# Attention and the first expert job on one core: transposes into two PSUM banks, other engines for some small steps, plain float32 in the first second layer

## The chip, the cores and the metric

The program runs on one core of one Trainium2 chip. Its time is the device time of one execution in microseconds (us), the median of several runs. Five engines work beside each other and wait for one another on semaphores: TensorE (PE in the rows; PEld is its weight load), VectorE (DVE), ScalarE (ACT), GpSimd (POOL) and SyncE (SP), which here only issues transfers.

## The reference

Three layers follow one another. Only the first, and the first job of the second, are touched by the change.

```
q, k, v: (4, 12, 448, 64) float32
q_n, k_n = rmsnorm(q, g_q), rmsnorm(k, g_k)
scores   = q_n @ k_n.T / 8;  attn = softmax(scores);  x = attn @ v     # -> (1792, 768)
expert   = argmax of x_n @ emb_n.T / tau, gate = its softmax weight    # 8 experts, top 1
x        = gate * relu(x @ w1[expert]) @ w2[expert]                    # w1: 768x1024, w2: 1024x768
out      = leaky_relu(x @ w_in) @ w_out                                # 768x2048, 2048x768, float64 weights
```

## The kernel before

All products are made to nearly float32 precision from a rounded part ("hi", type fp32r, one pass of TensorE) and a remainder ("lo"): hi*hi + hi*lo + lo*hi. Each value that enters a product is therefore copied once by ACT (hi = rounded copy) and subtracted once by DVE or POOL (lo = value - hi).

**Attention** runs over 12 pairs n (two heads, two batches) and 24 units u (one head of a pair, two batches side by side, so 896 rows of queries in seven tiles t of 128; tile 3 has 64 rows of either batch). For a pair: `load` brings q and k; `square`, `meansq`, `root` and `normalise` make the root mean square norm, mostly on POOL (the root itself is one `pow` on POOL, L280); `turn` (L322) transposes 16 tiles of 128x128 in four groups g (k and q of either batch) into PSUM tiles of one bank; `stack` makes hi (L335, L337) and lo (L339, L341) of each group; `swap` and `twice` (L352, L360) copy them by DMA so that hi and lo of a head lie above each other on 128 partitions. For the first pair the copies of the first head are made by ACT and DVE (`first_swap`, L381, L383), and unit 0 takes its third product from 64 partitions of `KL` alone (L413).

For a unit: `score` (L415) makes each tile with two products of 448 columns (four for tile 3), `rowmax` (L419, DVE) and `expo` (L425, ACT) follow; `ptrans` (L439) transposes the 28 blocks of the probabilities in eight groups g of four or three into one bank each, `psplit` makes hi (L450, ACT) and lo (L453, DVE) of each group; `pv` (L469) multiplies by v in 14 products; `evac` (L473, ACT) brings the two results to SBUF; `out_mm` (L489) turns them back and adds the expert logits, and `out_done` (L508, DVE) divides. PSUM has eight banks: two for scores, three for transposes (ring T), three for results (ring V).

**The order** of all this is written by a planner, `Order.run`: each operation has an engine, a price in ns, operations that it needs, rings of buffers that it takes and frees, and a due time (`TICKS`). The planner goes through a model of the five queues and writes the program in the order in which it would start the operations. An engine executes its instructions in that order, whatever the real times are.

**The first expert job** (`Experts.first`, also ordered by the planner) takes 128 tokens of expert 7 in four slices k of 256 hidden columns: `l1_parts` (L1204) makes x @ w1 in three parts, `relu`, a transpose (L1228), hi and lo (L1231, L1234), and `l2` (L1132, L1133) multiplies by w2 with three products per 128 hidden columns. Beside it run the routing of the second half of the tokens (L759 to L862), the gather of the rows of the next job (L1033) and their transposes (L1051). Splits of w1 and w2 run on ACT and DVE (L1015, L1017). The w1 of three slices is loaded during attention; the w2 of slices 1 to 3, and the w1 of slice 3, are loaded after attention has ended. The jobs after it (L1112 on) and the dense layer (L1626 on) have their own orders and are not touched.

Of the kernel before, what the change touches and what calls it, by code (L numbers as in the profile page):

```python
# [23 lines left out]
PS_T = 3  # L24
# [4 lines left out]
RAW = 3  # L29
TICKS = dict(start=1189.5, const=102.3, emb=15.4, max=0.4, exp=0.16, t=15.23, hi=5.93, lo=1.08, pv=30.06, ev=0.01,  # L30
             j=48.9, qk0=-40.65, qk1=-14.6, qk2=-23.81, qk3=-19.01, loadv=-29.18, v=-2.18, load=-67.34, norm=-54.47,
             root=16.77, mul=-14.43, route=2.68, droute=0.26, x0=-12.27)
# [6 lines left out]
ACTSQ = 3  # L39
WAIT = dict(PE=195, Act=140, DVE=125, Pool=70, SP=0)  # L40
# [60 lines left out]
class Attention:  # L101
    def __init__(self, tc, ctx, q, k, v, g_q, g_k, emb, tau, xtok, big, logits):
# [3 lines left out]
        self.xtok, self.big, self.logits = xtok, big, logits  # L106
# [10 lines left out]
        self.ps_v = pool("a_ps_v", 8 - PS_S - PS_T, space=PSUM)  # L117
# [4 lines left out]
    def setup(self, ident, turned):  # L122
        nc = self.nc
        self.ident, self.turned = ident, turned
# [3 lines left out]
        self.rhalf = c.tile([128, 28], F32, name="rhalf")  # L128
        nc.gpsimd.memset(self.rhalf, -0.5)
        self.KT = c.tile([128, 896], F32R, name="KT")  # L130
        self.QT = c.tile([128, 960], F32R, name="QT")
        self.QL = c.tile([128, 960], F32R, name="QL")
        for t in (self.QT, self.QL):
            nc.vector.memset(t[:, 448:512].bitcast(F32), 0.0)
        self.JE = c.tile([128, 12, 72], F32, name="JE")
        first = c.tile([128, 1], F32, name="first")
        nc.vector.memset(first, 0.0)
        nc.scalar.activation(out=first, in_=first, func=ACTF.Exp)

    def sums(self, half):  # L140

        rows = slice(half, half + 64)
        self.nc.scalar.copy(out=self.JE[rows, :, 0:64], in_=self.ident[rows, rows].unsqueeze(1).to_broadcast([64, 12, 64]))
# [13 lines left out]
    def zero_row(self):  # L157

        z = self.QT[:, 448:512].bitcast(F32)
# [3 lines left out]
    def experts(self, part):  # L163
# [20 lines left out]
        elif part == 4:  # L184
            self.emb_t = self.ps_t.tile([128, 512], F32, name="tp")
            for i in range(6):
                nc.tensor.transpose(self.emb_t[:, 8 * i:8 * i + 8], emb[:, 128 * i:128 * i + 128], self.ident[0:8, 0:8])
        else:
            je = self.JE.rearrange("p (i j) c -> p i j c", j=2)
            for a in (0, 64):  # L190
                for b in (0, 64):
                    nc.vector.tensor_copy(je[b:b + 64, :, a // 64, 64:72],
                                          self.emb_t[a:a + 64, 0:48].rearrange("p (i e) -> p i e", e=8))


    def load(self, n, i, part):
# [7 lines left out]
        if part == 1:  # L204
            for b in range(2):
                (nc.sync if n or i else nc.gpsimd).dma_start(out=qk[b * 64:b * 64 + 64, i + 6:i + 8, :],
# [6 lines left out]
    def load_v(self, n):  # L213
# [3 lines left out]
        vn = self.p1.tile([128, 16, 64], F32, name="vn")  # L217
        for b in range(2):
            nc.sync.dma_start(
                out=vn[:, b * 6:b * 6 + 6, :].rearrange("p (h r) d -> p h (r d)", r=3),  # L220
                in_=self.v[2 * bp + b, h0:h0 + 2, 0:384, :].rearrange("h (p r) d -> p h (r d)", r=3))
            for half in (0, 64):
                nc.sync.dma_start(
                    out=vn[half:half + 64, 12 + 2 * b:14 + 2 * b, :],
                    in_=self.v[2 * bp + b, h0:h0 + 2, 384:448, :].rearrange("h p d -> p h d"))
        self.pair[n]["vn"] = vn

    def split_v(self, n, part):
        nc = self.nc
        pr = self.pair[n]  # L230
        vn = pr["vn"]
        if part == 0:
            pr["vs"] = self.p2.tile([128, 16, 128], F32R, name="vs")
            nc.scalar.copy(out=pr["vs"][:, :, 0:64], in_=vn)
        else:
            s = slice(8 * part - 8, 8 * part)
            nc.gpsimd.tensor_tensor(out=pr["vs"][:, s, 64:128], in0=vn[:, s, :], in1=pr["vs"][:, s, 0:64].bitcast(F32),
# [9 lines left out]
    def square(self, n, a, b):  # L247
        nc = self.nc
        pr = self.pair[n]
        if "sq" not in pr:  # L250
            pr["sq"] = self.big("sq").rearrange("p (g d) -> p g d", d=64)
            for name in "ryzh":
                pr[name] = self.p2.tile([128, 28], F32, name="rstd" + name)
# [6 lines left out]
    def meansq(self, n, a, b):  # L260
# [4 lines left out]
        if n > 0:  # L265
# [6 lines left out]
    def root(self, n, a, b, k):  # L272
# [3 lines left out]
        if k > 11:  # L276
            if k == 12:
                self.nc.gpsimd.tensor_scalar(out=r, in0=r, scalar1=64e-6, scalar2=None, op0=ALU.add)
            else:
                self.nc.gpsimd.tensor_tensor(out=y, in0=r, in1=self.columns(self.rhalf, a, b), op=ALU.pow)  # L280
            return
# [25 lines left out]
    def turn(self, n, g):  # L307
# [4 lines left out]
        if g == 0:  # L312
            pr["KL"] = self.p2.tile([128, 896], F32R, name="KL")
        b, q = divmod(g, 2)
        base = 0 if q else 14
        ps = pr["t", g] = self.ps_t.tile([128, 512], F32, name="tp")
        o = 64 if g == 3 else 0

        last = [(base + 6, 0 if g == 3 else 384, self.turned if b else self.ident)]
        tiles = [(base + b * 8 + 2 * r, o + 128 * r, self.ident) for r in range(3)]  # L320
        for j, c, unit in last + tiles if g == 3 else tiles + last:
            nc.tensor.transpose(ps[:, c:c + 128], qk[:, j:j + 2, :].rearrange("p h d -> p (h d)"), unit)  # L322

    def stack(self, n, g, part):
        nc = self.nc
        pr = self.pair[n]
        ps = pr["t", g][:, 0:448]
        b, q = divmod(g, 2)
        if q:
            hi, lo = [t[:, 512 * b:512 * b + 448] for t in (self.QT, self.QL)]  # L330
        else:
            hi, lo = [t[:, 448 * b:448 * b + 448] for t in (self.KT, pr["KL"])]
# [1521 lines left out]
```

## Time and profile before

| | |
|---|---|
| median of 3 runs | 1159.12 us (1153.48 to 1159.16) |
| the profiled execution: its own time | 1154.31 us |
| its span, first to last instruction | 1152.4 us |
| TensorE busy | 1112.6 us, 97% |
| VectorE, ScalarE, GpSimd busy | 71%, 59%, 44% |
| attention, first score to last `out_mm` | 17.0 to 321.0 us |
| first expert job, to the first product of the next | 321.0 to 349.2 us |

How to read it: a busy PE is not PE at its peak, since the time of a product counts from its start to its modelled end, and products overlap. What a product costs in a stream is the step from one start to the next.

### The profile page before, as it was taken

The page shows a single profiled execution, that of the slowest core. Times are in us where ns is not written, and L with a number is a line of the kernel's source. Part 1 is how long each engine was busy: PE and PEld are TensorE (multiplying, and loading weights), DVE is VectorE, ACT ScalarE, POOL GpSimd, SP SyncE. Part 2 cuts the span into 40 slices and gives each one's busy share as a digit, 9 for nine tenths or more (in the row PEclk, how much of TensorE's full clock was granted, in tenths as well). Part 3 has the DMA queues.
Part 4 walks back from the last instruction along what each step waited for, and adds up shares of the span by engine and source line. Part 5 has one row for each costly group of instructions (what it writes and reads, how often), then busy time and mean ns, then how long its engine had stood idle before and what let it go on. Part 6 is the DMA issues. An engine that isn't in the chain of part 4 may idle for free. (4 is left out here: it accounts for less than half of the span.)

```text
span 1152.4 us, 19036 instructions
## 1 busy us (share of the span) xinstructions
PE 1112.6 (97%) x6863; PEld 985.0 (85%) x6863; DVE 813.1 (71%) x1354; ACT 681.3 (59%) x1346; POOL 501.4 (44%) x453
## 2 busy tenths in 40 slices
PE   5899999999989999999999999999999999999998
PEld 2789899899878999899899888888888888888997
DVE  5789898998877777877877779999933333323443
ACT  6889898799855665765856744544433332333453
POOL 6889898694211010201111156786683121221242
PEclk9999999999989999999999999999999999999999
DMA  7789988878487868977978655686543225323452
GB/s 156 168 187 216 203 204 191 182 175 213 129 278 262 302 227 285 328 249 259 359 254 282 221 193 207 204 300 241 213 165 138 97 80 180 110 83 109 166 192 83
DMA packets 155422, 233.09 MB, mean 202 GB/s; under 512 B 60286, under 2 KB 117886, under 8 KB 155326
## 3 DMA queue, kind: packets, MB, share of 16 engines
q1 hardware_dynamic: 151422, 215.75, 61.1%
q0 software_dynamic: 2784, 12.93, 3.5%
q10 hardware_dynamic: 1120, 3.16, 0.8%
q8 instruction: 56, 0.92, 0.3%
q14 instruction: 40, 0.33, 0.1%
HBM read 169.24 MB, written 30.81 MB: 174 GB/s over the span
## 5 line engine op out<-in xcount | busy, mean ns | idle before, releaser
L1604 POOL TENSOR_TENSOR w1l<-c,w1h 128x768 fp32r<-128x768 f32 x44 | 90.0, 2056 | 112.8 <-ACT w1h L1602 112.8
L1668 DVE SCALAR_TENSOR_TENSOR g<-hps,hs 128x512 f32<-128x512 f32 (+1 forms) x64 | 39.8, 621 | 134.9 <-ACT hs L1667 134.8
L1604 POOL TENSOR_TENSOR w2l<-c,w2h 128x768 fp32r<-128x768 f32 x42 | 88.6, 2119 | 91.7 <-ACT w2h L1602 87.6
L1667 ACT COPY hs<-hps 128x512 f32<-128x512 f32 (+1 forms) x64 | 34.1, 533 | 157.6 <-PE hps L1662 154.4
L419 DVE TENSOR_REDUCE negm<-S 128x1 f32<-128x448 f32 x165 | 101.5, 616 | 22.8 <-PE S L415 21.6
L1132 PE MATMUL ya<-w2h,QB 128*128 128x512 f32 x288 | 113.2, 404 | 0.5 <-ACT QB L1231 0.5
L425 ACT ACTIVATE P<-S,negm 128x448 f32<-128x448 f32 x165 | 105.4, 640 | 11.3 <-DVE negm L419 7.6
L450 ACT CAST PH<-tp 128x512 fp32r<-128x512 f32 (+1 forms) x192 | 98.2, 532 | 14.8 <-PE tp L439 13.6
L439 PE MATMUL tp<-ident,P 128*128 128x128 f32 (+1 forms) x672 | 105.3, 278 | 0.5 <-DVE PL L453 0.4
L1033 POOL DMA_INDIRECT KB<-rows,gidx x16 | 19.1, 1195 | 196.4 <-PE hps L1204 59.8
L1112 PE MATMUL hps<-xh,w1h 128*128 128x256 f32 x336 | 95.7, 285 | 1.2 <-ACT w1h L1015 1.2
L1112 PE MATMUL hps<-xh,w1l 128*128 128x256 f32 x336 | 95.1, 283 | 0.5 <-DVE w1l L1017 0.5
L1112 PE MATMUL hps<-xl,w1h 128*128 128x256 f32 x336 | 95.3, 284 | 0.3 <-DVE xl L1058 0.3
L439 PEld LDWEIGHTS tp<-ident,P 128*128 128x128 f32 (+1 forms) x672 | 81.8, 137 | 15.5 <-issue 1.3
L453 DVE TENSOR_TENSOR PL<-tp,PH 128x512 fp32r<-128x512 f32 (+1 forms) x144 | 86.8, 615 | 6.9 <-ACT PH L450 6.3
L1017 DVE TENSOR_TENSOR w1l<-qk,w1h 128x768 fp32r<-128x768 f32 x86 | 81.1, 956 | 13.9 <-ACT w1h L1015 13.5
L1669 ACT CAST gh<-g 128x512 fp32r<-128x512 f32 (+1 forms) x64 | 36.3, 568 | 81.1 <-DVE g L1668 80.2
L1133 PE MATMUL yb<-w2h,QB 128*128 128x256 f32 x288 | 81.8, 284 | 0.8 <-DVE yn L1179 0.8
L1662 PE MATMUL hps<-yh,w1h 128*128 128x512 f32 (+1 forms) x198 | 71.8, 363 | 0.1
L1662 PE MATMUL hps<-yh,w2h 128*128 128x512 f32 (+1 forms) x192 | 70.7, 368 | 1.1 <-DVE g L1668 1.1
L1662 PE MATMUL hps<-yh,w1l 128*128 128x512 f32 (+1 forms) x198 | 70.8, 358 | 0.0
L1662 PE MATMUL hps<-yl,w1h 128*128 128x512 f32 (+1 forms) x198 | 70.8, 357 | 0.0
(326 smaller groups left out, 3635.3 us busy)
## 6 DMA issues: line engine op xcount, KB each, us to landing
c<-wc SPq DMA_DIRECT2D x57, 768.0 KB, 4.6
qk<-in_moe_w SPq DMA_DIRECT2D x44, 768.0 KB, 6.8
x<-in_moe_w SPq DMA_DIRECT2D x27, 768.0 KB, 7.3
s<-in_moe_w_in SPq DMA_DIRECT2D x16, 768.0 KB, 7.7
s<-in_moe_w_out SPq DMA_DIRECT2D x16, 768.0 KB, 6.7
wc<-c SPq DMA_DIRECT2D x16, 768.0 KB, 6.1
LL<-KL SPq DMA_DIRECT2D x46, 224.0 KB, 4.5
sq<-in_moe_w SPq DMA_DIRECT2D x13, 768.0 KB, 7.4
```

Source lines behind the costliest of these rows:

```text
L419: self.nc.vector.tensor_reduce(out=un["negm"][:, t:t + 1], in_=un["S", t], op=ALU.max, axis=AXX, negate=True)
L425: self.nc.scalar.activation(out=un["P"][:, t, :], in_=un["S", t], func=ACTF.Exp, bias=un["negm"][:, t:t + 1], scale=1.0, accum_out=un["den ...
L439: nc.tensor.transpose(ps[0:m, 128 * j:128 * j + 128], P[:, t, 128 * c:128 * c + m], self.ident)
L450: nc.scalar.copy(out=hi, in_=ps)
L453: nc.vector.tensor_tensor(out=lo, in0=ps, in1=hi.bitcast(F32), op=ALU.subtract)
L1017: lo.tensor_tensor(out=t[2 * m + 1][:, s, :], in0=r, in1=hi.bitcast(F32), op=ALU.subtract)
L1112: nc.tensor.matmul(ps[:, 0:T], l, r, start=(a == 0), stop=(a == len(m) - 1))
L1132: nc.tensor.matmul(y["a"][j], l, r[:, 0:512], start=st, stop=sp)
L1133: nc.tensor.matmul(y["b"][j], l, r[:, 512:768], start=st, stop=sp)
L1604: eng.tensor_tensor(out=l, in0=c, in1=h.bitcast(F32), op=ALU.subtract)
L1662: nc.tensor.matmul(ps[:, t], l, r[:, t], start=(a == 0), stop=(a == len(m) - 1))
L1668: nc.vector.scalar_tensor_tensor(out=g, in0=ps[:, 0:T], scalar=0.01, in1=hs, op0=ALU.mult, op1=ALU.max)
```

## The change

- `turn`, `stack`, `ptrans` and `psplit` work on PSUM tiles of two banks: a pair has two groups of eight transposes instead of four of four, a unit four of seven instead of eight of four and three, and hi and lo are one instruction of up to 896 columns each. Ring T has two such tiles (four banks), ring V two banks. All transposes of a unit now need all seven tiles of its probabilities.
- The stacked q's have four fixed buffers with a zero gap; unit 0 takes its third product from a buffer `LL` of 128 partitions with zeros below, filled by two more DVE copies.
- `spin`: 23 products on zeros at the start, 3 and 1 more between the first transposes, whose result nobody reads.
- Other engines: the second evacuation of every odd unit from 5 on goes from ACT to DVE; the hi of v from ACT to POOL (not in pair 0); the mean squares and root of pair 1 from POOL to DVE; the root of pairs 2 to 11 is made in 3 steps on DVE and 12 on POOL instead of one `pow`, the second root chain of pair 0 in 12 steps on DVE.
- KT, QT, QL, v and small tiles now lie in the three buffers `p64`, which the w2 of the first job's slices takes over.
- First expert job: all four w1 and w2 slices are loaded during attention; `l2` of this job is one plain float32 product instead of three of fp32r, so its w2 and hidden values are no longer split.
- All prices and due times of the attention's planner are new.

```diff
-PS_T = 3
+PS_T = 2
+PS_V = 8 - PS_S - 2 * PS_T
+BUSY = 23, 3, 1
+EVAC = lambda u, b: "DVE" if u % 2 and b and u > 3 else "Act"
...
+        self.LL = [c.tile([128, 896], F32R, name=f"LL{hd}") for hd in range(2)]
+        nc.gpsimd.memset(self.LL[0][64:128, :].bitcast(F32), 0.0)
...
+        self.spin(BUSY[0])
...
+    def spin(self, n):
+        for _ in range(n):
+            self.nc.tensor.matmul(self.nothing, self.idle[:, 0:128], self.idle, start=True, stop=True)
...
-            nc.scalar.copy(out=pr["vs"][:, :, 0:64], in_=vn)
+            for b in range(2):
+                (nc.gpsimd.tensor_copy if n else nc.scalar.copy)(out=pr["vs"][:, 8 * b:8 * b + 8, 0:64], in_=self.vn[b])
...
-        if n > 0:
+        if n > 1:
             for w in (32, 16, 8, 4, 2):
                 nc.gpsimd.tensor_tensor(out=sq[:, :, 0:w], in0=sq[:, :, 0:w], in1=sq[:, :, w:2 * w], op=ALU.add)
...
-                self.nc.gpsimd.tensor_tensor(out=y, in0=r, in1=self.columns(self.rhalf, a, b), op=ALU.pow)
...
+        elif n > 1:
+            eng = self.nc.gpsimd
+            if k % 4 == 3:
+                eng.tensor_tensor(out=t, in0=y, in1=y, op=ALU.mult)
+            elif k % 4 == 0:
+                eng.tensor_tensor(out=t, in0=t, in1=h, op=ALU.mult)
+            elif k % 4 == 1:
+                eng.tensor_scalar(out=t, in0=t, scalar1=1.5, scalar2=None, op0=ALU.add)
+            else:
+                eng.tensor_tensor(out=y, in0=y, in1=t, op=ALU.mult)
...
-    def turn(self, n, g):
+    def turn(self, n, q, bs=range(2)):
...
+            pr["t", q] = self.ps_t.tile([128, 1024], F32, name="tp")
...
+        elif part == 1:
+            nc.vector.tensor_copy(t[64:128, c], (self.QL if q else self.KT)[0:64, c].bitcast(F32))
+        else:
+            nc.vector.tensor_copy(self.LL[0][0:64, c], self.pair[0]["KL"][0:64, c].bitcast(F32))
...
-            mm.append((Q[:, qc:qc + 128], pr["LL", hd][:, kc:kc + 448]) if u else
-                      (Q[rows, qc:qc + 128], KL[rows, kc:kc + 448]))
+            mm.append((Q[:, qc:qc + 128], self.LL[hd][:, kc:kc + 448]))
...
-        ps = un["t", g] = self.ps_t.tile([128, 512], F32, name="tp")
+        ps = un["t", c] = self.ps_t.tile([128, 1024], F32, name="tp")
         m = 128 if c < 3 else 64
-        for j, t in enumerate(range(4, 7) if half else range(4)):
-            nc.tensor.transpose(ps[0:m, 128 * j:128 * j + 128], P[:, t, 128 * c:128 * c + m], self.ident)
+        for t in range(7):
+            nc.tensor.transpose(ps[0:m, 128 * t:128 * t + 128], un["P"][:, t, 128 * c:128 * c + m], self.ident)
...
-                op(("max", u, t), "DVE", 531, x + D["max"], self.rowmax, (u, t), [("score", u, t)])
-                op(("exp", u, t), "Act", 611, x + D["exp"], self.expo, (u, t),
+                op(("max", u, t), "DVE", 616, x + D["max"], self.rowmax, (u, t), [("score", u, t)])
+                op(("exp", u, t), "Act", 843, x + D["exp"], self.expo, (u, t),
...
+        for k in range(4):
+            op(("pre64", k), "SP", 900, 17.0 * 24 - 20 + k, ex.preload2, (k,), [("swap", 11, h, j) for h in range(2) for j in range(2)] +
...
+    def preload2(self, k):
+        self.W.setdefault((0, k), {})
+        self.load2((0, k), self.w2[7], k)
...
-            m = [(hh[:, t], wh[:, fi, :]), (hh[:, t], wl[:, fi, :]), (hl[:, t], wh[:, fi, :])]
+            if key[0] == 0:
+                m = [(hs, w["r2"][fi])]
+            else:
+                (hh, hl), (wh, wl) = hs, w["t"][2:4]
+                m = [(hh[:, t], wh[:, fi, :]), (hh[:, t], wl[:, fi, :]), (hl[:, t], wh[:, fi, :])]
...
-                    op(("l2", k, fi), "PE", 960, X + D["l2"] + 1000 * fi,
+                    op(("l2", k, fi), "PE", 1280, X + D["l2"] + 1000 * fi,
```

## Rows read from the trace of the kernel before

**Rows 1.** Busy time of each engine by stage, granted clock, DMA share, GB/s.

```profile
17.00:28.00 11.00, 11.00 (x19) 4.86 (x19) 5.78 (x11) 7.53 (x17) 9.29 (x14) 1.00 0.88 184
28.00:40.00 12.00, 10.80 (x57) 8.85 (x56) 9.76 (x17) 10.79 (x25) 11.10 (x17) 1.00 0.58 136
40.00:60.00 20.00, 18.27 (x116) 15.92 (x115) 14.71 (x31) 15.36 (x37) 16.52 (x17) 0.91 0.88 191
60.00:300.00 240.00, 233.14 (x1601) 211.75 (x1600) 217.18 (x451) 210.50 (x532) 185.66 (x213) 1.00 0.87 199
300.00:321.00 21.00, 21.00 (x148) 19.48 (x147) 15.54 (x30) 14.35 (x36) 6.15 (x8) 1.00 0.10 32
321.00:349.20 28.20, 23.03 (x147) 20.14 (x146) 22.99 (x55) 16.53 (x30) 3.62 (x4) 0.88 0.99 329
```

**Rows 2.** Timeline of PE, late attention: start, us, what, [idle before <-releaser].

```profile
310.24 0.60 PE L439 MATMUL tp<-ident,P 128*128 128x128 f32 x4
310.60 0.45 PE L469 MATMUL O<-PH,vs 128*128 128x448 f32 x1
310.88 0.37 PE L469 MATMUL O<-PL,vs 128*128 128x448 f32 x1
311.09 0.60 PE L439 MATMUL tp<-ident,P 128*128 128x128 f32 x4
...
315.33 1.45 PE L489 MATMUL O<-JE,OT 128*128 128x72 f32 x12
316.58 0.45 PE L469 MATMUL O<-PH,vs 128*128 128x448 f32 x1
```

**Rows 3.** Timeline of PE, end of unit 0 and start of unit 1.

```profile
27.04 0.74 PE L415 MATMUL S<-KL,QA 64*128 64x448 f32 x1
27.71 2.82 PE L439 MATMUL tp<-ident,P 128*128 128x128 f32 x12
...
30.71 0.57 PE L415 MATMUL S<-LL,QB 128*128 128x448 f32 x1
31.08 0.57 PE L415 MATMUL S<-KB,QB 128*128 128x448 f32 x1
```

**Rows 4.** Timeline of ACT, the first exponential of unit 0.

```profile
20.64 0.62 ACT L425 ACTIVATE P<-S,negm 128x448 f32<-128x448 f32 x1
```

**Rows 5.** Timeline of DVE, one step of the first root chain.

```profile
9.77 0.18 DVE L294 SCALAR_TENSOR_TENSOR rstdy<-rstdz,rstdy 128x16 f32<-128x16 f32 x1
```

**Rows 6.** Waits of PE up to 330 us: total, times, longest.

```profile
PE S L415 <- DMA LL<-KL: 2.0, 2, 1.4
```

**Rows 7.** Groups by line and shape, 60 to 300 us: busy, mean ns | idle before.

```profile
L419 DVE TENSOR_REDUCE negm<-S 128x1 f32<-128x448 f32 x142 | 87.3, 616 | 15.6 <-PE S L415 14.5
...
L280 POOL TENSOR_TENSOR rstdy<-rstdr,rhalf 128x28 f32<-128x28 f32 x9 | 43.4, 4825 | 0.7
L453 DVE TENSOR_TENSOR PL<-tp,PH 128x512 fp32r<-128x512 f32 x61 | 41.0, 680 | 1.3 <-ACT PH L450 1.3
...
L450 ACT CAST PH<-tp 128x512 fp32r<-128x512 f32 x62 | 36.0, 591 | 6.2 <-PE tp L439 5.8
...
L453 DVE TENSOR_TENSOR PL<-tp,PH 128x384 fp32r<-128x384 f32 x60 | 31.9, 549 | 2.2 <-ACT PH L450 2.0
...
L450 ACT CAST PH<-tp 128x384 fp32r<-128x384 f32 x60 | 27.7, 477 | 1.3 <-PE tp L439 0.8
...
L473 ACT COPY OT<-O 128x448 f32<-128x448 f32 x40 | 21.6, 539 | 1.1 <-PE O L469 0.4 <-ACT PH L450 0.4
```

**Rows 8.** Timeline of PE in the first expert job.

```profile
336.78 0.40 PE L1132 MATMUL ya<-w2l,QB 128*128 128x512 f32 x1
...
337.13 0.40 PE L1132 MATMUL ya<-w2h,QB 128*128 128x512 f32 x1
...
349.19 0.39 PE L1112 MATMUL hps<-xh,w1h 128*128 128x256 f32 x1 [1.25 <-ACT w1h L1015]
```

**Rows 9.** Timeline of POOL: the gather for the next job is issued.

```profile
333.28 1.11 POOL L1033 DMA_INDIRECT KB<-rows,gidx  x1 [15.38 <-DVE gidx L857]
```

More of the change, by code (lines that the diff above doesn't have):

```diff
@@ L311, in turn, with stack @@
         qk = pr["qk"]
-        if g == 0:
+        if q == 0 and 0 in bs:
             pr["KL"] = self.p2.tile([128, 896], F32R, name="KL")
-        b, q = divmod(g, 2)
         base = 0 if q else 14
[L316 to L324, printed above, removed]
+        if ("t", q) not in pr or bs[0] == 0:
+            pr["t", q] = self.ps_t.tile([128, 1024], F32, name="tp")
+        ps = pr["t", q]
+        for b in bs:
+            tiles = [(base + b * 8 + 2 * r, 512 * b + 128 * r + 64 * q * b) for r in range(3)]
+            last = [(base + 6, (320, 512)[b] if q else (384, 832)[b])]
+            for j, c in last + tiles if b or q else tiles + last:
+                nc.tensor.transpose(ps[:, c:c + 128], qk[:, j:j + 2, :].rearrange("p h d -> p (h d)"), self.ident)
+        if n == 0 and (q, *bs) in ((1, 0), (0, 1)):
+            self.spin(BUSY[1 if q else 2])
+    def stack(self, n, q, part, bs=slice(0, 2)):
         nc = self.nc
         pr = self.pair[n]
[L327 to L332, printed above, removed]
+        both = lambda t, w: t.rearrange("p (b c) -> p b c", c=w)[:, bs, 0:448]
+        ps = both(pr["t", q], 512)
+        hi, lo = [both(t, 512 if q else 448) for t in ((self.QT, self.QL) if q else (self.KT, pr["KL"]))]
         if part == 0:
@@ L396, in score @@
         K = pr["KB"] if hd else pr["KA"]
-        KL = pr["KL"]
-        rows = slice(64 * hd, 64 * hd + 64)
         if t < 3:
@@ new lines, in run @@
+                op(("exp", u, t), "Act", 843, x + D["exp"], self.expo, (u, t),
+                   [("max", u, t)] + [("ptrans", u - 2, c) for c in range(4)], free=("V" if u < SPARE and t % 2 else "S", ("score", u, t)))
+            for c in range(4):
+                x = U + D["t"] + 17 * c / 4
+                op(("ptrans", u, c), "PE", 763, x, self.ptrans, (u, c), [("exp", u, t) for t in range(7)] +
+                   [("pv", u - 2, 1, 6)], take="T")
+                op(("phi", u, c), "Act", 925, x + D["hi"], self.psplit, (u, c, 0), [("ptrans", u, c)])
+                op(("plo", u, c), "DVE", 1086, x + D["lo"], self.psplit, (u, c, 1), [("phi", u, c)],
+                   free=("T", ("ptrans", u, c)))
@@ new lines, in run @@
+            for b in range(2):
+                for j, (c, lo) in enumerate(self.PV):
+                    x = U + D["pv"] + 17 * (7 * b + j) / 14
+                    op(("pv", u, b, j), "PE", 205, x, self.pv, (u, b, j), [("plo" if lo or c == 3 else "phi", u, c)] +
+                       [("v", n, 0), ("v", n, 1), ("v", n, 2), ("j", u - 2, 6)] + [("pv", u, b, j - 1)] * (j > 0),
+                       take=None if j else "V")
+                op(("ev", u, b), EVAC(u, b), 536, x + D["ev"], self.evac, (u, b), [("pv", u, b, j)],
+                   free=("V", ("pv", u, b, 0)))
@@ L1221, in turn_parts @@
         d = {}
-        hs = self.big("QA" if self.late else "QB").bitcast(F32R)
-        hh, hl = [hs[:, 256 * a:256 * a + 256] for a in range(2)]
+        hs = []
         def turn():
@@ L1230, in hi, with whole @@
         def hi():
[L1231 removed]
+            t = self.big("QA" if self.late else "QB").bitcast(F32R)
+            hs[:] = [t[:, 256 * a:256 * a + 256] for a in range(2)]
+            nc.scalar.copy(out=hs[0], in_=d["ps"][:, 0:256])
         def lo():
+            hh, hl = hs
             nc.vector.tensor_tensor(out=hl, in0=d["ps"][:, 0:256], in1=hh.bitcast(F32), op=ALU.subtract)
             return [(hh[:, 128 * a:128 * a + 128], hl[:, 128 * a:128 * a + 128]) for a in range(2)]
[L1237 removed]
+        def whole():
+            t = self.work.tile([128, 256], F32, name="hw")
+            nc.scalar.copy(out=t, in_=d["ps"][:, 0:256])
+            return [t[:, 128 * a:128 * a + 128] for a in range(2)]
+        return [turn, hi, lo, whole]
     def turn(self, h):
[L1240 removed]
+        return [f() for f in self.turn_parts(h)[0:3]][-1]
     def group(self, i):
@@ L1494, with __init__ @@
 class Dense:
-    def __init__(self, tc, ctx, ident, w_in, w_out, rows, slot, scratch, out):
+    def __init__(self, tc, ctx, ident, w_in, w_out, rows, slot, scratch, out, p64):
         self.tc, self.nc, self.ident = tc, tc.nc, ident
```

314 lines of the change are left out of this document (146 added, 168 removed).

## The prediction

> **What bounds the kernel now.** I read the stages first [rows 1]. The reader is to see that TensorE is the engine that sets the time from 60 us on: it is busy for 233.1 of 240.0 us between 60 and 300, while VectorE has 217.2 and ScalarE 210.5. GpSimd is well below with 185.7. So a microsecond taken from VectorE or ScalarE in that stage is worth nothing by itself; only TensorE's steps and its 6.9 us of idleness count. Three other stretches are worse. From 17 to 40 us TensorE looks busy but executes 76 products in 23 us, against 6.7 a microsecond later on. From 40 to 60 it is idle for 1.7 us and its granted clock is 0.91. From 321 to 349.2, the first expert job, it is busy for 23.0 of 28.2 us, the clock is 0.88, and the DMA engines are full (0.99), whereas in the 21 us before they are nearly empty (0.10).
>
> Then the timeline, for the steps. Late in attention four transposes and the product behind them take 310.24 to 310.88, and the next product, not behind transposes, 0.21 [rows 2]. So a product of 448 columns is 0.205 and a transpose (0.64 - 0.205) / 4 = 0.109; a little `out_mm` step is 1.25 / 12 = 0.104. A unit has 16 score products, 14 of `pv`, 28 + 8 transposes and 14 small steps: 6.15 + 3.92 + 1.46 = 11.5 us. That is the whole of it: the four groups instead of eight take away no work of TensorE. All 24 units need 277 us, and from 17 to 321 us there are 304. What can be gained in attention lies in that difference.
>
> **The change, part by part.**
>
> *Unit 0.* Its last steps are 0.67 each for 448 columns [rows 3]; unit 1's, directly after, are 0.37, later ones 0.205. The granted clock is printed as 1.00 here, but 0.37 against 0.205 says that TensorE runs at the lower of its two levels (1.2, not 2.4 GHz) until after 31 us. The further step from 0.37 to 0.67 belongs to unit 0's alternation of 64 and 128 rows, which no other unit has. The change ends the alternation: 16 x 0.30 = 4.8 us of TensorE. The spins may raise the clock before the first scores: 16 x 0.165 = 2.6 more, and some 12 x 0.10 + 4 x 0.165 = 1.9 on the steps up to 31.5, so 9.3 at most. But the first exponential starts only at 20.64 [rows 4], since ScalarE is still making operands, and from 17 to 40 ScalarE is idle for only 3.5 + 1.2 = 4.7 us [rows 1]. VectorE is idle for 5.2 + 2.2 = 7.4 us there and gets the mean squares of pair 1 (1792 columns, four times the 448 of a `rowmax`: 4 x 0.616 = 2.5 [rows 7]), twelve root steps of 0.18 [rows 5] and two copies to LL (about 0.3 each by the planner's price): 5.3 us. It fits, barely. The twelve steps of the second root chain of pair 0 (2.2 us on VectorE, ahead of its own copies) can make the first score up to 1 us later. I take 4 us gained, bounds 0 and 9.3.
>
> *40 to 60 us.* One wait for LL is 1.4 us long [rows 6], and the clock falls around it; 9% of 20 us is 1.8 us of full clock. The pair-1 norm no longer passes through the long `pow` on GpSimd (4.83 us each [rows 7]), so these operands come earlier. I take 2 us, bounds 0 and 3.5 (idle time plus clock).
>
> *60 to 300 us.* ScalarE loses per unit the fixed part of four casts: now 4 x (0.591 + 0.477) = 4.27 us [rows 7], later four of 896 columns. 128 columns cost the difference of 0.114, so 896 cost 0.93, and the saving is 4 x 0.14 = 0.55. VectorE's remainders go the same way: 0.131 per 128 columns, 1.07 instead of 1.23, saving 0.64. It gets ten evacuations (0.539 on ScalarE now) and three small root steps a pair; both stay under TensorE. GpSimd loses a 4.83 us `pow` a pair and gets twelve small steps and two copies: between 12 x 0.1 and 12 x 0.4 us plus less than the 1.28 us that it needs for each subtraction of v today, so it does not become the bound at 185.7 of 240. None of this moves the end unless it removes the 6.9 us of idleness, or adds to it: the transposes have two slots instead of three. I take 0, bounds 6.9 gained and 17 lost (rival below).
>
> *300 to 321 us.* TensorE is full and has the same products: 0. The loads that come in here (three w2 slices and one w1, 3.1 MB, beside the one w2 that was already early) find the DMA engines at 0.10. On SP they now stand ahead of the last stores of x and of the logits, for which the gather waits; the fourth w1 waits for a buffer that GpSimd's split of slice 0 frees, and would hold these stores up only if that came after 321, which I cost at nothing.
>
> *First expert job.* Of 28.2 us, TensorE is busy for 23.0, of which the clock's 12% are 3.4: 19.6 us of work at full clock. Its queue is filled with w loads (DMA share 0.99) while the gather of the next job's rows, issued at 333.28 [rows 9], and w1's first cast, awaited until 349.19 [rows 8], hold the end. With 3.1 of some 9.3 MB (28.2 us at 329 GB/s) loaded before, and with eight casts and eight subtractions of w2 gone from ScalarE and VectorE, both come earlier. Against this stands plain float32. A product with 768 columns steps by 337.13 - 336.78 = 0.35, so three rounds are 1.05. No row shows a wide plain float32 product; `out_mm` is one, and appears as two records per product. From below it is two rounds, 0.70. From above, a float32 transpose steps by 0.109 per 128 columns [rows 2], so twelve of them, two records of 768 columns, are 1.31. I take the upper end, the one from a row in float32: 8 x 0.26 = 2.1 us more work, a floor of 21.7 us, at most 6.5 gained; from the other side, nothing comes earlier and 2.1 are lost. I take 5, since what held the stage was late data, and most of that lateness was the DMA share.
>
> The Trainium skill (FP8 and Floating Point Precision, TensorE Precision Notes) says that true float32 goes through the array in four passes. By it a product is 4 x 0.35 = 1.40, the eight cost 2.8 more instead of 2.1, and the sum below would be 0.7 higher. No row before shows it; the profile after will.
>
> **The sum.** 1154.3 (the profiled execution) - 4 - 2 + 0 - 5 = 1143.3. The median of the runs shown is 4.8 above that execution, since two of three runs are at 1159.1 and one at 1153.5, so a little of that may be in the median after: I say 1144.
>
> **Rivals.** *Two slots for transposes.* A slot is held for 7 x 0.109 + 0.93 + 1.07 = 2.8 us before any wait. Each of cast and remainder can stand behind one exponential (0.62 [rows 4]) or one `rowmax` (0.616 [rows 7]), which makes 4.0. Five uses a unit through two slots are then 10.0 us of the 11.5, and before, ten uses of (0.38 + 0.53 + 0.61 + 1.24) = 2.8 through three slots were 9.2. For it: the margin falls from 2.3 to 1.5 us, and each unit's first transpose now waits for all seven exponentials. Against it: ScalarE has more air, and TensorE has scores and `pv` to put between. It decides from a further 0.6 us of waiting per use (5 x 4.6 / 2 = 11.5). At 0.7 us of stall a unit, 24 x 0.7 = 17 us, the time is 1160: slower.
>
> *VectorE takes back what TensorE gains.* The head's 5.3 us on VectorE fall into the maxima of units 0 and 1, and unit 2 is no earlier than now. Then only the expert job gains: 1154.3 - 5 = 1149, within half a per cent of before. For it: 5.3 of 7.4 us idle; against it: part of that work fits before 17 us.
>
> *All waits go.* The head gives 9, the stretch to 60 3.5, the steady stage its 6.9, the job 6.5: 1154.3 - 25.9 = 1128. For it: TensorE's 277 us of work in attention would still have 285. Against it: three engines between 88% and 97% seldom run without waits.
>
> **How the numbers follow.** Half a per cent (5.8 us) is about what this measurement can tell from no change. Chances: the forecast 0.60 (its own range is 1136 to 1149), two slots 0.17, VectorE 0.12, all waits 0.11. The range that leaves out no more than 2 in 10 runs from 1130, near the third rival, to 1158, which leaves out the worst of the first: 1130 to 1158. Faster: 0.60 + 0.11 less a little of the forecast's upper end, 0.69. Same: 0.15. Slower: 0.16, the first rival less its mild cases.
>
> **What would show it.** Unit 0's products step by 0.37 or 0.205 instead of 0.67, and unit 2's scores start before 44 us. Between 60 and 300 the same product count takes TensorE as long as before within 5 us; waits of L439's successor for remainders would speak for two slots. After attention, DMA share well under 0.99, the gather issued and landed earlier, and the next job's first product less than 24 us after the last `out_mm`. Wide plain float32 products at 1.3 us a slice half. The prediction is wrong if TensorE's idle time in attention grows by more than 8 us, or if the spins delay the first transposes beyond 12 us.

## The result, and the profile after

The kernel after takes 1171.53 us (median of 4 runs, 1168.67 to 1175.03); the kernel before took 1156.86 beside it. The ratio is 1.0132, 95% interval 1.0106 to 1.0159: 1.3% slower, some 15 us, and outside the predicted range. The profiled executions lie further apart, by 20.8 us (spans 1173.2 and 1152.4).

The stages after, read as [rows 1]: busy time of PE, PEld, DVE, ACT and POOL with instruction counts, then the granted clock, DMA share and GB/s. Attention now ends at 347.3 instead of 321.0 us, and the job's stage lasts to 370.3.

```profile
17.00:28.00 11.00, 7.52 (x25) 5.79 (x25) 9.76 (x26) 7.51 (x18) 3.31 (x5) 0.66 0.74 159
28.00:40.00 12.00, 8.95 (x41) 7.57 (x41) 9.89 (x20) 9.08 (x20) 8.18 (x15) 0.63 0.80 186
40.00:60.00 20.00, 14.04 (x70) 10.69 (x69) 15.07 (x34) 13.03 (x27) 15.37 (x38) 0.74 0.81 167
60.00:180.00 120.00, 115.57 (x776) 104.91 (x775) 107.06 (x177) 94.18 (x199) 106.22 (x189) 1.00 0.82 192
180.00:200.00 20.00, 16.49 (x103) 14.99 (x102) 12.74 (x22) 12.04 (x27) 14.04 (x27) 0.91 0.79 184
200.00:240.00 40.00, 38.07 (x261) 33.75 (x260) 36.51 (x65) 31.24 (x67) 31.19 (x54) 1.00 0.72 171
240.00:260.00 20.00, 15.41 (x87) 13.68 (x86) 17.02 (x33) 11.47 (x24) 9.90 (x19) 0.83 0.71 178
260.00:300.00 40.00, 39.67 (x275) 36.87 (x273) 33.90 (x52) 31.76 (x69) 8.71 (x14) 1.00 0.77 187
...
347.30:370.30 23.00, 20.90 (x135) 16.34 (x134) 17.40 (x45) 11.88 (x23) 3.26 (x3) 1.00 0.86 283
```

The reader is to see three holes: everything to 60 us (136 products from 17 us on, where before had 192), 180 to 200, and 240 to 260. Elsewhere TensorE is nearly as full as before. To size them I weigh each recorded product by its step at full clock [rows 2] (0.205, transposes 0.109, `out_mm` 0.104) and add up. The fifteen small products of the routing count as 0.205 too, which is more than they are: before, all of them fall into 200 to 240, after, seven into 240 to 260.

| us of work done by TensorE | before | after |
|---|---|---|
| to 60 us | 29.1 | 25.3, of which 5.5 are spins |
| 60 to 180 | 114.4 | 112.4 |
| 180 to 200 | 19.8 | 14.7 |
| 200 to 240 | 38.4 | 37.8 |
| 240 to 260 | 20.1 | 12.4 |
| 260 to 300 | 38.7 | 39.3 |

So 9.3 us are lost to 60 us, 5.1 and 7.7 in the two later holes (the last is 9.2 without the routing's products), 2.0 from 60 to 180: 24 of the 26.3 by which attention ends later.

The waits of TensorE from 17 to 321 us after (total, times, longest):

```profile
PE S L456 <- ACT P L466: 6.8, 7, 3.5
PE tp L479 <- DVE PL L491: 4.7, 7, 2.0
PE S L456 <- DMA QA<-s: 3.5, 1, 3.5
PE O L456 <- DVE QA L424: 3.4, 1, 3.4
PE S L456 <- DVE KA L424: 3.3, 1, 3.3
PE tp L362 <- DVE PL L491: 2.5, 5, 1.0
PE S L456 <- DMA LL<-KL: 1.7, 1, 1.7
```

Before, the same stretch has, beside the 2.0 of [rows 6], two of more than 1 us:

```profile
PE S L415 <- ACT P L425: 3.6, 4, 1.9
PE S L415 <- DMA QA<-QL: 2.8, 1, 2.8
```

Unit 0's steps (PE timeline; [rows 3] had 0.67) are 0.37, but behind a wait of 3.35 us, so its last score starts at 27.30, against 27.04 before. Unit 2's first score waits 3.46 us for the copy of QA of pair 1. The products with v (L506) begin only at 60.5 us, against 36.4 before, because POOL makes the second remainder of v of pair 0 at 58.16:

```profile
24.55 0.71 PE L456 MATMUL O<-KA,QA 128*128 128x448 f32 x1 [3.35 <-DVE QA L424]
...
25.43 0.57 PE L456 MATMUL S<-KA,QA 128*128 128x448 f32 x1
25.81 0.57 PE L456 MATMUL S<-LL,QA 128*128 128x448 f32 x1
...
27.30 0.57 PE L456 MATMUL S<-LL,QA 128*128 128x448 f32 x1
...
49.30 0.71 PE L456 MATMUL S<-KA,QA 128*128 128x448 f32 x1 [3.46 <-DMA QA<-s]
...
60.50 0.37 PE L506 MATMUL O<-PH,vs 128*128 128x448 f32 x1
```

```profile
58.16 1.28 POOL L271 TENSOR_TENSOR vs<-s,vs 128x512 fp32r<-128x512 f32 x1
```

The hole at 184 us, timelines of POOL and of DVE: a late load of q holds POOL's mean squares, and a root step that is now on DVE (L311) waits for them with the maxima behind it.

```profile
184.10 1.68 POOL L290 TENSOR_TENSOR sq<-qk 128x896 f32<-128x896 f32 x1 [6.01 <-DMA qk<-in_q]
```

```profile
189.25 0.18 DVE L311 TENSOR_SCALAR s<-s 128x28 f32<-128x28 f32 x1 [4.79 <-POOL s L302]
189.34 0.62 DVE L460 TENSOR_REDUCE negm<-S 128x1 f32<-128x448 f32 x1
```

The costs of the casts and remainders of 896 columns were right (0.93 and 1.07 us expected from [rows 7]), in the groups by line: busy time, mean ns of one.

```profile
L488 ACT CAST PH<-tp 128x896 fp32r<-128x896 f32 x96 | 86.6, 902 | 20.0 <-PE tp L479 19.4
...
L491 DVE TENSOR_TENSOR PL<-tp,PH 128x896 fp32r<-128x896 f32 x72 | 77.9, 1082 | 1.5 <-ACT PH L488 1.3
```

The first expert job after ([rows 8] of before): plain float32 products (two records each) of 768 columns step by 355.14 - 353.85 = 1.29 us, and the next job's first product is at 370.25, 23.0 us after attention's end (28.2 before). TensorE is idle for 2.1 us of this stage, where before it was for 5.2.

```profile
353.85 1.02 PE L1188 MATMUL ya<-s,hw 128*128 128x512 f32 x2
354.71 0.59 PE L1189 MATMUL yb<-s,hw 128*128 128x256 f32 x2
355.14 1.02 PE L1188 MATMUL ya<-s,hw 128*128 128x512 f32 x2
...
370.25 0.36 PE L1164 MATMUL hps<-xh,w1h 128*128 128x256 f32 x1
```

### The profile page after: what moved, and what is told of

It is laid out like the page before. It is cut to its first block, busy times and chain, and to the rows that moved or that the text cites. A ratio compares the mean times of both kernels' runs of the same rounds, so it can differ in the third digit from the quotient of the medians.

```text
span 1173.2 us, 18923 instructions
## 1 busy us (share of the span) xinstructions
PE 1123.4 (96%) x6874; PEld 995.6 (85%) x6874; DVE 822.2 (70%) x1298; ACT 657.8 (56%) x1202; POOL 476.3 (41%) x557
## 5 line engine op out<-in xcount | busy, mean ns | idle before, releaser
L1188 PE MATMUL ya<-w2h,QB 128*128 128x512 f32 x272 | 106.4, 402 | 0.5 <-ACT QB L1289 0.5
L479 PE MATMUL tp<-ident,P 128*128 128x128 f32 (+1 forms) x672 | 93.6, 282 | 9.4 <-DVE PL L491 5.7
L479 PEld LDWEIGHTS tp<-ident,P 128*128 128x128 f32 (+1 forms) x672 | 79.1, 138 | 22.8 <-PE S L456 10.7
L488 ACT CAST PH<-tp 128x896 fp32r<-128x896 f32 x96 | 86.6, 902 | 20.0 <-PE tp L479 19.4
L491 DVE TENSOR_TENSOR PL<-tp,PH 128x896 fp32r<-128x896 f32 x72 | 77.9, 1082 | 1.5 <-ACT PH L488 1.3
L1189 PE MATMUL yb<-w2h,QB 128*128 128x256 f32 x272 | 77.1, 283 | 0.8 <-DVE yn L1235 0.8
L1067 ACT CAST w1h<-qk 128x768 fp32r<-128x768 f32 x86 | 69.9, 829 | 4.6 <-DVE lt L1204 4.6
L506 PE MATMUL O<-PH,vs 128*128 128x448 f32 x192 | 71.3, 384 | 0.0
```

The source lines that it names most:

```text
L479: nc.tensor.transpose(ps[0:m, 128 * t:128 * t + 128], un["P"][:, t, 128 * c:128 * c + m], self.ident)
L488: nc.scalar.copy(out=hi, in_=ps)
L491: nc.vector.tensor_tensor(out=lo, in0=ps, in1=hi.bitcast(F32), op=ALU.subtract)
L1188: nc.tensor.matmul(y["a"][j], l, r[:, 0:512], start=st, stop=sp)
L1189: nc.tensor.matmul(y["b"][j], l, r[:, 512:768], start=st, stop=sp)
```

## The experiments

"Planned anew" means that the edit changes what the planner sees, so that the whole order of attention may differ. Ratios are to the kernel before, run beside; after has 1.0132.

**Attention or job?** The old attention with the new job and the moved buffers. Of the diff, the lines that move the buffers:

```diff
-        self.KT = c.tile([128, 896], F32R, name="KT")
...
+        raw = [self.p64.tile([128, 768, 2], I32, name="s64").bitcast(F32).rearrange("p d w -> p (d w)") for _ in range(3)]
+        self.KT, self.QT, self.QL = [t[:, 0:w].bitcast(F32R) for t, w in zip(raw, (896, 960, 960))]
```

> This is the kernel before with its own attention (one-bank transposes, three slots, its prices and due times, its norm), the buffers of the kernel after (KT, QT, QL, v in the three p64 buffers) and the first expert job of the kernel after. Theory A, the new attention alone costs the time and the job gains what was forecast: the job takes 23 us instead of 28.2 and attention its old 304, so 1157 - 5 = 1152 (1149 to 1154). Rival, the moved buffers and the early loads of w2 cost attention its time: 1165 or more.

Measured 1150.28 us, ratio 0.9943 (0.9924 to 0.9963). Attention ends at 320.4, the next job starts 24.9 us later:

```profile
320.40:345.30 24.90, 21.81 (x133) 16.95 (x132) 17.30 (x45) 10.82 (x22) 3.04 (x3) 0.93 0.87 287
```

The new job and the moved buffers cost nothing, and all of the loss belongs to the new attention. The medians gain 5.1 us; in this profile 3.3 of them are the job's, where 5 were forecast. This version beats both kernels, by 0.6% the one before.

**Removing the visible waits, one at a time.** The root by one `pow` on GpSimd in the same place of the order:

```diff
+        if n > 1:
+            if k == 3:
+                self.nc.gpsimd.tensor_scalar(out=r, in0=r, scalar1=64e-6, scalar2=None, op0=ALU.add)
+            elif k == 4:
+                self.nc.gpsimd.tensor_tensor(out=y, in0=r, in1=self.columns(self.rhalf, a, b), op=ALU.pow)
+            return
```

> The kernel after, with the root of pairs 2 to 11 as one add and one pow on GpSimd again; order of everything else unchanged. Theory A (VectorE's queue stands behind the three root steps when the mean squares are late): the stall of 184 to 190 us and half of that of 244 to 252 go, 5 to 8 us: 1164 to 1167. Rival B (two slots for transposes are too few, wherever the root is made): within 2 us of 1171.5.

Measured 1181.35, ratio 1.0213 (1.0191 to 1.0235): 10 us slower than after. The hole at 184 us is gone (142 products from 180 to 200 instead of 103), but GpSimd's longer `pow` makes v's remainders late, and TensorE waits 3.3 us for one of them.

The same for pair 1's mean squares and root and pair 0's second chain (condition `n == 1 or (n == 0 and a == 36)`, and `meansq` on GpSimd for n > 0):

> The kernel after, with the mean squares and the root of pair 1 and the second root chain of pair 0 on GpSimd again (pow), order unchanged. Theory A (VectorE's queue is what holds the head): the waits of TensorE for the copies to KA and QA (3.3 and 3.4 us) go, the head gains 5 us: 1166 or 1167. Rival C (the order holds it: ring T gives its two slots to pair 1 before unit 0's transposes): nothing gained, and pair 1, later by its 4.8 us pow, loses 0 to 4 us: 1171 to 1176.

Measured 1171.96, ratio 1.0136 (1.0116 to 1.0155): nothing. The waits for KA and QA are still 2.8 and 3.3 us, so the norm's steps on VectorE are not what makes them. What does make them is not shown.

Without spins:

```diff
-BUSY = 23, 3, 1
+BUSY = 0, 0, 0
```

> The kernel after without the 27 products on zeros. If the spins raise the clock for the first scores, their absence costs the 16 products of unit 0 up to 0.165 us each: up to 2.6 us, 1174. If the clock falls anyway in the gaps before them, as the granted clock's row says (half from 13.1 to 19.9 us): no change, 1171.5 within 1.5.

Measured 1171.68, ratio 1.0134 (1.0115 to 1.0153): the spins are worth nothing here.

Pair 0's v early:

```diff
-            op(("loadv", n), "SP", 3900, N + D["loadv"], self.load_v, (n,), [("v", n - 1, 1), ("v", n - 1, 2)], after=2000)
...
+            op(("loadv", n), "SP", 3900, N + (D["loadv"] if n else -29.18), self.load_v, (n,), [("v", n - 1, 1), ("v", n - 1, 2)], after=2000)
...
-                op(("v", n, k), "Pool", 1230, N + D["v"], self.split_v, (n, k), [("v", n, 0)], after=200)
+                op(("v", n, k), "Pool", 1230, N + (D["v"] if n else -2.18), self.split_v, (n, k), [("v", n, 0)], after=200)
```

> The kernel after, with the load and the splits of v of pair 0 given the due times that they have in the kernel before (-29.18 and -2.18 instead of 4.17 and 87.74); the planner makes the order anew. In the kernel after v's last remainder of pair 0 is made at 58.2 to 59.4 us and the first product with v is at 60.5 (before: 36.4), so TensorE has nothing to put between the scores of units 0 to 2. Theory D (this late v is the loss of the head): products of v start before 45 us, the 9 us that TensorE's work is behind at 60 us shrink to 3 or less, and the time falls by 5 to 9: 1163 to 1166. Rival (VectorE and ScalarE limit the head, whatever TensorE is given): the order is different, the work done at 60 us more but the scores later, and the time within 2 of 1171.5.

Measured 1178.88, ratio 1.0216 (1.0193 to 1.0239). TensorE does 27.6 instead of 25.3 us of work to 60 us, but now waits 7.3 us for a copy of QA, and the new order has other holes later.

The root of pairs 2 to 11 wholly on GpSimd, and both together:

```diff
-        eng = self.nc.vector
+        eng = self.nc.gpsimd if n > 1 else self.nc.vector
```

> The kernel after, with all 15 root steps of pairs 2 to 11 on GpSimd (3 small steps of 0.2 us a pair more there, none on VectorE), the planned order unchanged. Moving the root to one pow removed the stall of 184 to 190 us, but each pow is 1.9 us longer than the steps and v's remainders came late behind it. Theory A (a root step on VectorE that waits for late mean squares stops the maxima behind it): the stall at 184 us goes and nothing else comes, 5 us from there and 1 to 3 from 244 to 252 us: 1164 to 1167. Rival: GpSimd, late anyway, passes its lateness on by another way, as with pow: 1170 or more.

> The kernel after with both: pair 0's v early, the root of pairs 2 to 11 all on GpSimd; planned as with v early alone. If the two causes are separate their gains add: 10 to 16 us, 1156 to 1162, which is the kernel before again. If the second is only a chance of the old order, it adds nothing: the time of early v alone.

Measured 1177.36, ratio 1.0180 (1.0152 to 1.0209), and 1179.13, ratio 1.0213 (1.0193 to 1.0232). In the first of them the hole at 184 us shrinks (122 products instead of 103), the one at 240 us grows (73 instead of 87). Theory A, that VectorE's queue is the cause, forecast a gain of 5 to 8 us, and none came: its stall is real, but no way tried of mending it gives time.

**The slots and banks, in the old attention.** Two one-bank slots for transposes (and four banks for results), then four (and two banks for results):

```diff
-PS_T = 3
+PS_T = 2
```

> The attention of the kernel before with the new first job (1150), but with two one-bank slots for transposes instead of three (four banks for results): the price of the slot count by itself, planned anew. Rival B (two slots are too few): 0.7 us a unit or more, 1165 or later. If the slot count isn't what costs: 1150 to 1154.

Measured 1197.42, ratio 1.0362 (1.0336 to 1.0388): 47 us slower than with three.

> The attention of the kernel before with the new first job (1150), with four one-bank slots for transposes and two banks for results: the same four plus two banks that the kernel after has, in one-bank pieces. If the two banks for results are what costs: 1165 or more. If they are enough: 1148 to 1154, and what costs in the kernel after is that its four banks are only two pieces.

Measured 1161.61, ratio 1.0061 (1.0040 to 1.0082): 11 us slower. So two banks for results are not enough, even where the transposes have four slots. Its windows of the products with v alone (L476; busy PE, PEld) show the place: the routing of the first half takes a result bank at 207.6 us, and from 218 to 225 no product with v runs. By the weights above TensorE does 33.9 us of work from 200 to 240, where the version with three and three banks does 38.7. A further wait, of 3.1 us for a copy of QA at 269 us, has another place, so not all of the 11 us is put down to the bank.

```profile
207.00:218.00 11.00, 2.23 (x7) 1.24 (x7) 1.00 0.83 179
218.00:225.00 7.00, 0.00 (x0) 0.00 (x0) 0.76 0.73 163
225.00:245.00 20.00, 8.68 (x30) 5.51 (x30) 1.00 0.63 145
```

**The two-bank transposes alone.** From after, the norm, v, the evacuations and the spins are put back as before; due times of after, then of before:

```diff
-EVAC = lambda u, b: "DVE" if u % 2 and b and u > 3 else "Act"
+EVAC = lambda u, b: "Act"
...
-        if n > 1:
+        if n > 0:
...
-                for k in range(15 if n > 1 else 12):
+                for k in range(12) if n == c == 0 else (12, 13):
```

> The kernel after with everything of its attention undone except the two-bank transposes (with their splits in one instruction), the fixed buffers and their two plus two bank rings: the norm as before (mean squares of pairs 1 to 11 and every pow on GpSimd), v's hi and all evacuations on ScalarE, no spins. Due times of the kernel after, planned anew. If the two-bank form with its coarser hand-over is what costs (B): 1168 or more in this and in the next run. If the moved small steps on VectorE and GpSimd cost (A): near 1152.

> The same with the due times of the kernel before, as far as they have a counterpart (those of the four groups of q and k averaged in pairs). If the due times cost (C), one of these two runs is 10 us faster than the other and near 1155; if the two-bank form costs (B), both are at 1168 or more.

Measured 1184.84, ratio 1.0261 (1.0235 to 1.0287), and 1192.58, ratio 1.0329 (1.0306 to 1.0352): slower than after. So with these orders the moved small steps, taken together, are not what the two-bank form costs. One of them, the split root, harms the old attention when it is put there (the diff is to the first version above):

```diff
-                for k in range(12) if n == c == 0 else (12, 13):
+                for k in range(15) if n > 1 else range(12) if n == c == 0 else (12, 13):
```

> The attention of the kernel before with the new first job (1150), with the root of pairs 2 to 11 in 3 steps on VectorE and 12 on GpSimd as in the kernel after; planned anew. Theory A (a root step on VectorE that waits for late mean squares stops the maxima): 5 us or more slower, 1155 or later. If only an attention without spare slots suffers from it: 1148 to 1152.

Measured 1171.07, ratio 1.0143 (1.0121 to 1.0166), 21 us slower than with `pow`; TensorE waits 5.2 us for QB and 4.7 for QA there, operands that come from the norm.

**Is it only the order?** The change's prices are near the spans of the trace. On ACT an exponential and the read of its sum are 0.63 + 0.19, near the price of 843, but the next exponential starts 0.63 after the last (ACT timeline of after):

```profile
28.40 0.63 ACT L466 ACTIVATE P<-O,negm 128x448 f32<-128x448 f32 x1
28.93 0.19 ACT L466 ACTIVATION_READ_ACCUMULATOR P<-O,negm 128x1 f32 x1
29.03 0.64 ACT L466 ACTIVATE P<-S,negm 128x448 f32<-128x448 f32 x1
```

```diff
-                op(("max", u, t), "DVE", 616, x + D["max"], self.rowmax, (u, t), [("score", u, t)])
+                op(("max", u, t), "DVE", 531, x + D["max"], self.rowmax, (u, t), [("score", u, t)])
-                op(("exp", u, t), "Act", 843, x + D["exp"], self.expo, (u, t),
+                op(("exp", u, t), "Act", 611, x + D["exp"], self.expo, (u, t),
...
```

> The kernel after, with the planner's prices of nine operations set to the steps that the trace shows (exponential 611 instead of 843, maximum 531 for 616, cast of probabilities 787 for 925, remainder 998 for 1086, out_done 660 for 825, reciprocal 108 for 190, evacuation 414 on ScalarE and 531 on VectorE for 536, the casts and remainders of q and k); no instruction is changed, only the order. Theory E (the order was planned with prices that are too high, so that TensorE is given gaps it need not have): 8 to 15 us faster, 1157 to 1163. Rival B (two slots cost the time in any order): 1168 to 1180.

> The same prices, with due times looked for anew so that the planned end of attention is early. Theory E: attention as short as before or nearly, 1150 to 1156. Rival B: two coarse slots leave 10 us or more: 1162 or later.

Measured 1170.07, ratio 1.0126 (1.0095 to 1.0157), and 1165.01, ratio 1.0079 (1.0051 to 1.0107). The prices by themselves give nothing that can be told from no change, with new due times 6 us. Yet in the profile with the prices alone one of the three holes is closed and another smaller: the first product with v is at 41.5 us, 31.9 us of work are done to 60 us (spins included), and 135 products run from 180 to 200. In part the loss has moved (109.8 us of work from 60 to 180 instead of 112.4), so the size of a hole is not what closing it is worth. The reverse in the old attention, and a control there (pv 31.06 for 30.06):

> The attention of the kernel before with the new first job (1150), planned with the change's prices for the exponential (843 instead of 611) and the maximum (616 for 531); no instruction is changed. Theory E: 10 us or more slower, 1160 to 1172. Rival B: three finer slots forgive it: within 5 of 1150.

> The attention of the kernel before with the new first job (1150), with one due time moved by 1 (pv 31.06 instead of 30.06): a control for what a new order without any reason costs. If orders are much alike: 1148 to 1153. If the due times before are a lucky point: 1155 to 1165, and all differences of that size between kernels planned anew tell little.

Measured 1163.02, ratio 1.0063 (1.0039 to 1.0087), and 1151.54, ratio 0.9970 (0.9951 to 0.9990). Span prices cost the old attention 13 us; a new order without a reason cost 1 to 3, in the one control there is.

**The held bank.** In after, routing's first product is at 232.22 and its table is read at 254.10 (timelines of PE and DVE). Products with v (L506) in these windows after, where before 18 ran while its routing held one of three banks (215 to 226 us, the row by itself):

```profile
232.22 0.20 PE L838 MATMUL O<-offb,ones 1*128 1x56 bf16 x1
254.10 0.27 DVE L909 COPY table<-O 128x112 f32<-128x112 f32 x1
```

```profile
208.00:232.00 24.00, 6.59 (x25) 4.04 (x24) 1.00 0.69 168
232.00:241.00 9.00, 3.50 (x12) 1.92 (x12) 1.00 0.86 205
241.00:256.00 15.00, 0.01 (x1) 0.00 (x0) 0.77 0.78 196
```

```profile
215.00:226.00 11.00, 5.33 (x18) 3.09 (x18) 1.00 0.91 197
```

The same shows in the other profiles. Between routing's first product and the read of its table, 14 to 30 us, there are 4 to 11 products with v in the twelve versions that hold one of two result banks all that time, and 13 to 19 in the six with three or four banks.

The edit gives the bank back after the first read and takes another for the seven table products, which it also moves behind all one-hot rows:

```diff
+                if a == 0 and bp == 0:
+                    s["ps"] = psum()
...
+        steps.insert(pe[2] - 1, steps.pop(pe[1]))
+        pe[1] = pe[2] - 1
...
-            ring = dict(take="V") if k == pe[0] else dict(free=("V", ("route", pe[0]))) if k == len(steps) - 2 else {}
+            ring = dict(take="V") if k in pe[0:2] else {}
+            if k in (pe[0] + 1, len(steps) - 2):
+                ring = dict(free=("V", ("route", pe[0] if k == pe[0] + 1 else pe[1])))
```

> The kernel after with step prices (1170), and the routing of the first half takes a result bank twice for a short time instead of once for about 22 us: the bank goes back after the first read, and a new one is taken for the seven table products, which now follow one another after all one-hot rows are made. The same work otherwise. Theory V (one of only two result banks is held by the routing, so products with v stop): the 6 to 8 us that TensorE's work loses between 240 and 260 us come back, 1162 to 1164. Rival (VectorE's routing steps, not the bank, make that gap): 1168 to 1172.

Measured 1162.53, ratio 1.0043 (1.0026 to 1.0059), 7.5 us less than with the same prices and due times without the edit (1170.07). From routing's first product to the read of the table 23 products with v run in 16.5 us, where without the edit 8 run in 14.1 (24 in 20.2 us in the last version below, which has the short hold too). In the window in which after had one, it has 14, but without the edit there are 12 already:

```profile
241.00:256.00 15.00, 4.15 (x14) 2.40 (x14) 1.00 0.65 180
```

TensorE's work from 240 to 260 us is 18.3 us instead of 11.8 without the edit. But without the edit TensorE also waits 4.9 us in its queue at the table products (L902), for VectorE's one-hot rows (L880):

```profile
PE O L902 <- DVE sq L880: 4.9, 3, 3.0
```

With the table products moved behind the rows, this wait is gone too. So it is shown that the held bank stops the products with v, also in the old attention, where two result banks make such a hole. That it alone costs the 7.5 us is not shown: the rival, VectorE's routing steps, can have a large part of them, and no run has the short hold without the moved products. In after itself TensorE has no such wait at the table products; it waits there for remainders and probabilities, 4.6 us from 240 to 258.

> The two-bank transposes alone as in the run with the new due times (norm as before, v and evacuations on ScalarE, no spins; 1185), with step prices, the short hold and due times looked for anew. If the order was what made the two-bank form slow (prices, due times, the held bank): 1150 to 1156, like the old attention. If two coarse slots cost in any order (B): 1160 or more.

Measured 1173.37, ratio 1.0147 (1.0116 to 1.0178): 11 us faster than that form with the first due times, and not like the old attention. Its waits from 60 to 320 us are for operands, not for slots:

```profile
PE S L464 <- DMA QA<-s: 6.2, 3, 2.4
PE S L464 <- DMA QB<-s: 4.4, 1, 4.4
PE S L464 <- ACT P L474: 2.9, 5, 1.6
```

By what was expected this speaks for B (1160 or more). But the due times are one choice among many, so it doesn't show that two coarse slots must cost time, nor that they need not.

## Why the prediction was wrong

*The step that failed* is "60 to 300 us ... I take 0". I counted work per engine and the slots for transposes, and left out the other half of the edit of PSUM: the result ring falls from three banks to two. TensorE's work there falls short by 15 us, and its idle time from 17 to 321 us grows from 9.8 to 27.3, well over the 8 that the prediction named as its sign of being wrong. The 15 are inside my bounds (17 lost), but the bounds came from the slots for transposes, not from this ring. 7 to 8 of the 15 are lost in a hole in which the routing of the first half holds one of the two banks for 22 us: 11 products with v run in that time, where before, with three banks, 18 ran in 17.5 us. That the held bank stops them is shown. What it costs at the end is not: 7.5 us came back when the hold was shortened, but together with TensorE's wait for the one-hot rows. The other visible piece, 5 us at 184, is a wait that the change adds on VectorE (a root step behind a late load); I had costed the three steps as busy time only, and not asked who is queued behind them. Three attempts to take it away gained nothing, and the step prices closed the hole without gaining time, so its share of the end is not shown.

*Head (4 and 2 us gained)*: this failed too, and outside its bounds of no loss: TensorE does 9 us less there. Unit 0's steps were read rightly (0.37 instead of 0.67), but a wait of 3.35 us for its operands took the gain back. That "these operands come earlier" was wrong for pair 1: TensorE waited 3.46 us for a copy of QA, and unit 2's scores began at 49.3, not before 44 (47.3 before). I left the due times out. That of pair 0's v moved from -2 to 88, and TensorE had no product with v to put between the scores until 60 us; but with the same due time and step prices it has one at 41.5, so it is not the due time by itself. The granted clock was 0.63 to 0.74 from 17 to 60 us (its two levels of 1.2 and 2.4 GHz by turns, before 0.91 to 1.00). v early alone gave no time, so this is a description of the head and not a proven price. The spins changed nothing.

*First expert job (5 us)*: right in size, 5.2 in the profile; 3.3 in the profile of the run that has it without the new attention, whose median is 5.1 lower. The float32 product took 1.29 us, by the bound from the float32 transposes 1.31. The estimate of 1.40, from the four passes that the Trainium skill states for true float32 (FP8 and Floating Point Precision, TensorE Precision Notes), is 0.11 too long here; the measurement decides. The clock was 1.00 instead of 0.88 and the DMA share 0.86 instead of 0.99. The gather was issued only a little earlier, 11.3 us after attention's end instead of 12.3, so most of the gain is elsewhere: TensorE waited 3.1 us for casts of w1 before (`ACT w1h`), and not at all after.

*The rivals.* "Two slots for transposes" gave the sign, and it isn't ruled out: TensorE waits 7.2 us for remainders in all of 17 to 321, but an order planned for two slots can lose time without a wait that shows. Two one-bank slots do cost 47 us in the old attention, more than that rival's 17; two-bank ones alone, with the orders tried, 23 to 42 against 1150. "VectorE takes back the head's gain" had it right that unit 2 is no earlier, and two of the waits there are for VectorE's copies; but with the norm's steps back on GpSimd nothing was gained. "All waits go" did not happen.

*What stays open*: some 12 us between the best two-bank version (1162.5) and the old attention (1150.3). Due times alone move such versions by 5 to 8 us (1170 to 1165, 1185 to 1193), so a part may be tuning; the short hold and the better due times were not run together in the kernel after. Whether the coarse slots have a price of their own isn't settled.

## What to carry to other kernels

When a pool of PSUM is divided anew, count both sides of the division, and look for the rare user that holds a bank for long: here one of two banks was gone for 14 to 22 us once in a kernel, and a shorter hold, with the products that end it moved behind their operands, gave back 7.5 us. An order that is planned from prices wants the step between consecutive instructions, not the span that a trace shows for each (611 against 843 ns for the exponential): in an attention that was otherwise unchanged the wrong ones cost 13 us, though putting them right in the two-bank form gave nothing by itself. In a full pipeline, mending one visible wait proves nothing until the time falls: five such edits here, each aimed at a real wait, gave nothing or a loss. And an edit that removes two things at once prices neither.

## What the runs showed of the hardware

A `pow` on GpSimd over 28 values a partition is 4.83 us long and still served the old attention better than 3 steps on VectorE and 12 of 0.23 to 0.28 us on GpSimd (1150 against 1171 us); that this is the hand-over between two queues is argued, not shown. Small steps on VectorE that read only SBUF took far longer while GpSimd worked on large tiles: a one-hot row of 112 columns 1.33 us at 240.54, beside GpSimd's remainders of v, and 0.32 at 243.79, when GpSimd was idle.
